# k features of the later batches in 64-row by 32-column tiles of the TensorE array, one matmul for all token tiles, products kept by head pair

## The chip, the cores and the metric

One core of a Trainium2 chip runs the whole program. The metric is device time in microseconds (us), the median of several executions. A profile is taken of one of these executions; its span is about 1.8 us shorter than the time of that execution.

Engine names in the profile: PE is the TensorE matmul, PEld its weight load, DVE is VectorE, ACT is ScalarE, POOL is GpSimd, SP issues most of the DMA. "L256" is line 256 of that kernel's file; the same statement has other line numbers in other versions.

Names in the traces: "pg" and "po" are the results of the matmuls with w_in and w_out, "g" is the square between them, "kvp" collects v^T kp and the sums of kp, "ks" is VectorE's sum of kp over the first eight token tiles, "qT" is q transposed. A "wave" is a group of matmul records that start within a few ns of each other.

## The reference, cut to what matters

```python
batch, n_heads, seq, head_dim = 4, 4, 1088, 32          # r = 8
def phi(x):
    a = einsum('rd,bhsd->bhsr', S1, x)                  # 8 features a
    b = einsum('rd,bhsd->bhsr', S2, x)                  # 8 features b
    return einsum('bhsi,bhsj->bhsij', a, b).reshape(..., 64)
q_p, k_p = phi(q), phi(k)
kv = einsum('bhsf,bhsd->bhfd', k_p, v);  z = k_p.sum(2)
attn = einsum('bhsf,bhfd->bhsd', q_p, kv) / (einsum('bhsf,bhf->bhs', q_p, z)[..., None] + 1e-6)
x = attn as (4352, 128);  h = relu(x @ w_in);  out = (h * h) @ w_out    # w_in 128x2048
```

The feed-forward part (FFN) is by far the larger. Attention for batches 1 to 3 is worked in between its matmuls. This is about one small piece: the features a and b of k ("kf"), their transposes ("fs") and their products ("kp").

## The kernel before: the parts that matter

k lies in `kq`, transposed in blocks of 32: the partitions are the four heads times 32 dimensions, the columns are tokens, `32 * NT = 288` for each of four token groups `p0`. `sk` holds S1 and S2 as block-diagonal weights: head h has rows 32h to 32h+31 and 8 columns of each half.

```python
KG = [[(0, 2), (2, 2), (4, 2), (6, 3)]] + [[(0, 4), (4, 5)]] * (B - 1)   # token tiles per group

def a_kf(b, g, pool, tag):                # batch > 0
    t0, n = KG[b][g]
    kf = pool.tile([128, 512], F32, tag=tag, name="kf")      # one PSUM bank for each token group
    for i in range(2):                    # features a, then features b
        for p0 in range(4):               # four column tiles of the array
            nc.tensor.matmul(
                kf[32 * p0 : 32 * p0 + 32, 32 * n * i : 32 * n * i + 32 * n],
                sk[:, 32 * i : 32 * i + 32],                              # 128 rows x 32 columns
                kq[:, 32 * (NT * p0 + t0) : 32 * (NT * p0 + t0 + n)],
            )
# a_fs: DVE transpose kf -> fs;  a_kp: DVE product kp = a x b, one tile per token group
# [... cut ...]
def a_kf2(b):
    a_kf(b, 0, psa, "feat")               # two banks
    a_kf(b, 1, psa, "tr")

def a_kv(b, t):                           # kvp += v^T kp, token tile t; the last tile has 64 rows
    n, v0, dv = (128, 512 * (t // 4) + 32 * (t % 4), 128) if t < 8 else (64, 1024, 32)
    for h in range(H):
        nc.tensor.matmul(st[b, "kvp"][32 * h : 32 * h + 32, 0:64], vn[b][0:n, ...], kp[0:n, ...], ...)

def loads(n):                             # DMA for batch n, during batch n - 1
    load_qk(kn[n], k, n, 0, S)
    for part in range(3):
        load_v(vn[n], n, part)
    load_qk(qn[n], q, n, 0, S)
```

A small list planner puts every attention task into a numbered FFN step, from estimated durations.

## Time and profile before

| | before |
|---|---|
| time, median of 3 | 202.68 us (202.6 to 203.17) |
| span of the profile | 200.7 us |
| PE busy | 193.1 us (96%) |
| one kf block (from the end of the w_out stream before it to the first FFN matmul after it) | 1.21 us, three times |

From the page of the kernel before: the span, the busy times (engine, us, share, instructions), and the chain of work that ended last, by engine and by line.

```profile
span 200.7 us, 3928 instructions
...
PE 193.1 (96%) x1329; PEld 125.1 (62%) x1329; DVE 143.7 (72%) x375; ACT 144.7 (72%) x326; POOL 50.4 (25%) x225
...
PE 84%; DMA 6%; DVE 3%; ACT 2%; SPq 1%; issue 1%; ACTq 0%
PE po L512 54%; PE pg L489 14%; PE nd L388 7%; DMA w_in_100<-in_moe_w_in_dram 4%; PE qc L362 3%; DMA vn<-in_v_dram 2%; PE kvp L299 2%; PE pt L529 2%; PE kf L256 2%; ACT gt L498 1%; SPq L104 1%; DVE qa L372 1%; PE kvp L310 1%; ACT w_in L684 1%; DVE qp L377 0%
```

PE is the limit. What shares of the chain do not show is whether a microsecond saved on a line is saved at the end. For that one looks for PE gaps after the line: after 20 us there are almost none but those around changes of tile shape. In windows around the three blocks (us, length, then the busy time of PE, PEld, DVE, ACT and POOL with their instructions, the granted clock and the DMA) PE is busy throughout:

```profile
30.00:46.00 16.00, 16.00 (x169) 9.44 (x168) 13.47 (x27) 13.29 (x30) 3.11 (x18) 1.00 0.11 19
...
72.00:88.00 16.00, 16.00 (x169) 9.33 (x168) 14.16 (x30) 12.54 (x28) 0.00 (x0) 1.00 0.25 57
118.00:134.00 16.00, 16.00 (x170) 9.43 (x169) 14.61 (x31) 12.60 (x28) 0.00 (x0) 1.00 0.15 27
```

The chain in order of time (start, us, what) has the three kf blocks:

```profile
33.51 1.12 PE kf L256 x32
...
75.70 1.12 PE kf L256 x32
...
121.29 1.12 PE kf L256 x32
```

The timeline of PE around the first of them (start us, us, what; a merged group starts at its first record):

```profile
32.70 0.81 PE L512 MATMUL po<-g_576,w_o 128*128 128x384 f32 x2
33.44 1.19 PE L256 MATMUL kf<-kq,sk 128*32 128x128 f32 x32
34.56 0.34 PE L489 MATMUL pg<-xT,w_in 128*128 128x384 f16 x1
```

"128*32" is the tile of the array. Each fp32 matmul is two records, so 16 matmuls are 32 records. The groups of instructions that the change touches (count | busy us, mean ns of one | idle before):

```profile
L256 PE MATMUL kf<-kq,sk 128*32 128x160 f32 x48 | 2.2, 299 | 0.0
...
L256 PE MATMUL kf<-kq,sk 128*32 128x128 f32 x48 | 1.9, 279 | 0.0
```

```profile
L282 DVE TENSOR_TENSOR kp<-fs 128x1280 f32<-128x1280 f32 x3 | 4.4, 1483 | 0.0
...
L282 DVE TENSOR_TENSOR kp<-fs 128x1024 f32<-128x1024 f32 x3 | 3.6, 1194 | 0.0
...
L275 DVE STREAM_TRANSPOSE fs<-kf 128x320 f32<-128x320 f32 x3 | 1.5, 499 | 0.0
L275 DVE STREAM_TRANSPOSE fs<-kf 128x256 f32<-128x256 f32 x3 | 1.3, 428 | 0.0
```

The 299 and 279 ns of a kf record are no cost per matmul: four of them run at once and the next four follow 109 or 136 ns later. Costs of packed matmuls are read from the starts of single records.

### The profile page before, as it was taken

The numbers are of one execution on the slowest core, as the hardware profiler recorded it, in microseconds if no ns is written. First come the engines' busy times: TensorE is split into PE (matmuls) and PEld (weight loads), VectorE is DVE, ScalarE is ACT, GpSimd is POOL, SyncE is SP. The second block draws the span as 40 slices with busy tenths as digits, with TensorE's granted clock in tenths as the row PEclk, the third lists the DMA queues.
The fourth block names the chain that finished last, engine by engine and source line by source line (L and its number), as shares of the span: only waits on it lengthen the run. The fifth ranks groups of instructions, "written<-read, shape, count | busy, mean of one in ns | idle before, by whom it ended". The sixth has DMA issues, their size and how long they took to land.

```text
span 200.7 us, 3928 instructions
## 1 busy us (share of the span) xinstructions
PE 193.1 (96%) x1329; PEld 125.1 (62%) x1329; DVE 143.7 (72%) x375; ACT 144.7 (72%) x326; POOL 50.4 (25%) x225
## 2 busy tenths in 40 slices
PE   7998999999999999999999999999999999999990
PEld 2873765567667655667676655667676655556990
DVE  3966966896497669984767788984667767667750
ACT  3428988977696877796978777786888766756730
POOL 3815056000426800001654400000653500000000
PEclk9999999999999999999999999999999999999997
DMA  6699410110120571020112660020122010110201
GB/s 187 184 271 284 141 49 20 20 23 0 23 39 20 164 204 20 2 44 0 36 32 45 207 150 0 3 39 0 23 43 39 2 33 0 22 21 0 39 0 33
DMA packets 31357, 12.34 MB, mean 61 GB/s; under 512 B 23338, under 2 KB 29930, under 8 KB 31338
## 3 DMA queue, kind: packets, MB, share of 16 engines
q1 hardware_dynamic: 30886, 12.00, 24.1%
q8 instruction: 10, 0.16, 0.3%
q10 hardware_dynamic: 452, 0.10, 0.3%
q14 instruction: 9, 0.07, 0.1%
HBM read 8.78 MB, written 2.23 MB: 55 GB/s over the span
## 4 chain that ended last, share of the span: by engine, by line
PE 84%; DMA 6%; DVE 3%; ACT 2%; SPq 1%; issue 1%; ACTq 0%
PE po L512 54%; PE pg L489 14%; PE nd L388 7%; DMA w_in_100<-in_moe_w_in_dram 4%; PE qc L362 3%; DMA vn<-in_v_dram 2%; PE kvp L299 2%; PE pt L529 2%; PE kf L256 2%; ACT gt L498 1%; SPq L104 1%; DVE qa L372 1%; PE kvp L310 1%; ACT w_in L684 1%; DVE qp L377 0%
## 5 line engine op out<-in xcount | busy, mean ns | idle before, releaser
L498 ACT ACTIVATE gt<-pg 128x384 f32<-128x384 f32 (+2 forms) x193 | 88.7, 463 | 34.8 <-PE pg L489 34.0
L544 POOL COPY br<-beta 32x3 f32<-32x3 f32 x192 | 43.5, 227 | 104.4 <-DVE beta L452 97.1
L489 PE MATMUL pg<-xT,w_in 128*128 128x384 f16 (+2 forms) x193 | 61.1, 316 | 0.5 <-ACT gt L498 0.2
L489 PEld LDWEIGHTS <-w_in 128*128 128x128 f16 x193 | 18.9, 98 | 19.1 <-issue 1.4
L372 DVE STREAM_SHUFFLE qa<-qc 128x384 f32<-128x384 f32 x22 | 12.0, 589 | 0.0
L388 PEld LDWEIGHTS nd<-kvz_120,qp 128*128 128x128 f32 x72 | 10.0, 190 | 3.1 <-DVE qp L377 0.3
L388 PEld LDWEIGHTS nd<-kvz_119,qp 128*128 128x128 f32 x72 | 9.9, 190 | 2.5
L377 DVE TENSOR_TENSOR qp<-qa,qb 128x384 f32<-128x384 f32 x22 | 11.2, 544 | 0.0
L552 DVE STREAM_TRANSPOSE oT<-po 128x384 f32<-128x384 f32 (+1 forms) x11 | 6.2, 564 | 6.4 <-PE po L512 6.3
L282 DVE TENSOR_TENSOR kp<-fs 128x512 f32<-128x512 f32 (+3 forms) x10 | 10.7, 1104 | 0.1
L388 PE MATMUL nd<-kvz_120,qp 128*128 128x132 f32 x72 | 10.3, 277 | 0.1
L388 PE MATMUL nd<-kvz_119,qp 128*128 128x132 f32 x72 | 10.0, 277 | 0.0
L404 DVE TENSOR_SCALAR den<-nd 128x12 f32<-128x12 f32 x12 | 2.0, 169 | 10.8 <-PE nd L388 10.7
L362 PE MATMUL qc<-qT,sq 128*128 128x384 f32 x22 | 8.8, 489 | 0.0
L445 DVE TENSOR_TENSOR xs<-nd,sc 128x384 f16<-128x384 f32 (+2 forms) x13 | 6.7, 522 | 0.4
L367 DVE STREAM_SHUFFLE qb<-qc 128x384 f32<-128x384 f32 x11 | 6.5, 588 | 0.0
L299 PE MATMUL kvp<-kp,vn 128*32 128x64 f32 (+1 forms) x288 | 6.3, 222 | 0.0
L299 PEld LDWEIGHTS kvp<-kp,vn 128*32 128x32 f32 (+1 forms) x288 | 4.9, 109 | 2.2 <-DVE ks L322 0.5
L240 DVE STREAM_TRANSPOSE qT<-qn 128x1088 f32<-128x1088 f32 (+2 forms) x5 | 5.3, 1057 | 1.3 <-DMA qn<-in_q_dram 1.3
L409 DVE TENSOR_REDUCE mx<-nd 128x12 f32<-128x384 f32 x12 | 5.9, 495 | 0.0
L362 PEld LDWEIGHTS qc<-qT,sq 128*128 128x128 f32 x22 | 4.1, 190 | 2.8
L558 DVE TENSOR_TENSOR ob<-oT,br 128x384 f32<-128x384 f32 (+1 forms) x11 | 5.8, 530 | 0.0
(702 smaller groups left out, 404.0 us busy)
## 6 DMA issues: line engine op xcount, KB each, us to landing
vn<-in_v_dram SPq DMA_DIRECT2D x32, 64.0 KB, 3.4
kn<-in_k_dram SPq DMA_DIRECT2D x3, 544.0 KB, 7.9
qn<-in_q_dram SPq DMA_DIRECT2D x3, 544.0 KB, 3.6
out_dram<-ob SPq DMA_DIRECT2D x32, 48.0 KB, 1.8
w_in_100<-in_moe_w_in_dram SPq DMA_DIRECT2D x2, 512.0 KB
w_o<-in_moe_w_out_dram SPq DMA_DIRECT2D x2, 512.0 KB, 10.7
out_dram<-ob SPq DMA_DIRECT2D x12, 40.0 KB, 2.6
qn<-in_q_dram SPq DMA_DIRECT2D x1, 352.0 KB
```

The source lines that it names most:

```text
L282: nc.vector.tensor_tensor(out=_ap(kp, 0, 128, 0, [[64, 4 * n], [8, 8], [1, 8]]), in0=_ap(fs, 0, 128, 0, [[8, 4 * n], [1, 8], [0, 8]]), in1 ...
L299: nc.tensor.matmul(st[b, "kvp"][32 * h : 32 * h + 32, 0:64], _ap(vn[b], 0, n, v0 + dv * h, [[1, 32]]), kp[0:n, c0 + 64 * h : c0 + 64 * h + ...
L362: nc.tensor.matmul(qc[:, 0:384], sq[:, :], qT[:, 384 * ch : 384 * ch + 384])
L367: nc.vector.stream_shuffle(in_=st[b, "qc", ch][:, 0:384], out=qb[:, :], mask=mask_b)
L372: nc.vector.stream_shuffle(in_=st[b, "qc", ch][:, 0:384], out=qa[:, :], mask=mask_a[e])
L377: nc.vector.tensor_tensor(out=qp[:, :], in0=st[b, "qa", ch, e][:, :], in1=st[b, "qb", ch][:, :], op=mult)
L388: nc.tensor.matmul(nd[:, 132 * o : 132 * o + 132], st[b, "qp", ch, e][:, 128 * o : 128 * o + 128], st[b, "kvz"][:, 132 * e : 132 * e + 132 ...
L445: nc.vector.tensor_tensor(out=_ap(st[b, "xs", ch], 0, 128, 128 * o, [[32, 4 * n], [1, 32]]), in0=_ap(st[b, "nd", ch], 0, 128, 132 * o, [[3 ...
L489: nc.tensor.matmul(pg[:, c0:c1], w_in[:, 128 * c : 128 * c + 128], st[b, "xT"][:, 384 * ch + c0 : 384 * ch + c1],)
L498: nc.scalar.activation(gt[:, c0:c1], pg[:, c0:c1], Relu)
L512: nc.tensor.matmul(st["po", b, ch][:, c0:c1], w_o[:, 128 * c : 128 * c + 128], g2s[i][1][:, c0:c1], start=first, stop=(c == NFF - 1), skip ...
L544: nc.gpsimd.tensor_copy(_ap(st[b, "br"], 32 * dm, 32, 12 * ch + p0, [[4, 3]]), st[b, "beta"][32 * p0 : 32 * p0 + 32, 3 * ch : 3 * ch + 3],)
```

## The change

Each kf matmul of a later batch contracts over 128 rows although a head needs only 32 of them; the rest of the weights are zeros. The change cuts the array into two row halves as well: heads 0 and 1 in rows 0 to 63, heads 2 and 3 in rows 64 to 127. A half gives 2 heads x 16 = 32 feature columns, one column tile. The banks now belong to head pairs instead of token groups; all nine token tiles go into one matmul of 288 columns, and kp is laid out by head pair. S1 and S2 are interleaved column by column in `sk`, so that a pair's columns are contiguous.

```diff
-    KG = [[(0, 2), (2, 2), (4, 2), (6, 3)]] + [[(0, 4), (4, 5)]] * (B - 1)
+    KG = [[(0, 2), (2, 2), (4, 2), (6, 3)]]
@@ weights
-            _ap(sk, 32 * h, 32, 8 * h, [[32, 2], [1, 8]]),
+            _ap(sk, 32 * h, 32, 16 * h, [[1, 2], [2, 8]]),
@@ a_kf, batch > 0
-            for i in range(2):
-                for p0 in range(4):
-                    nc.tensor.matmul(
-                        kf[32 * p0 : 32 * p0 + 32, 32 * n * i : 32 * n * i + 32 * n],
-                        sk[:, 32 * i : 32 * i + 32],
-                        kq[:, 32 * (NT * p0 + t0) : 32 * (NT * p0 + t0 + n)],
-                    )
+            for p0 in range(4):
+                nc.tensor.matmul(
+                    kf[32 * p0 : 32 * p0 + 32, 0 : 32 * NT],
+                    sk[64 * g : 64 * g + 64, 32 * g : 32 * g + 32],
+                    kq[64 * g : 64 * g + 64, 32 * NT * p0 : 32 * NT * (p0 + 1)],
+                )
@@ products, batch > 0: one tile kp2, by head pair, a and b read at a step of two
+        nc.vector.tensor_tensor(
+            out=_ap(st[b, "kp2"], 0, 128, 128 * NT * g, [[64, 2 * NT], [8, 8], [1, 8]]),
+            in0=_ap(fs, 0, 128, 0, [[16, 2 * NT], [2, 8], [0, 8]]),
+            in1=_ap(fs, 0, 128, 1, [[16, 2 * NT], [0, 8], [2, 8]]),
+            op=mult,
+        )
@@ planner estimates
-        P.add(("kf", n), "PE", 1.2, need, a_kf2, n)
+        P.add(("kf", n), "PE", 0.6, need, a_kf2, n)
[... cut: planner estimates of fs and kp, addresses of kp in kvp and in the ks sums, batch 0's copies at a step of two ...]
```

More of the change, by code (lines that the diff above doesn't have):

```diff
@@ L242, in a_kf @@
     def a_kf(b, g, pool, tag):
-        t0, n = KG[b][g]
+        t0, n = KG[b][g] if b == 0 else (0, NT)
         kf = pool.tile([128, 512], F32, tag=tag, name="kf")
@@ L252, in a_kf @@
         else:
-            for i in range(2):
-                for p0 in range(4):
-                    nc.tensor.matmul(
-                        kf[32 * p0 : 32 * p0 + 32, 32 * n * i : 32 * n * i + 32 * n],
-                        sk[:, 32 * i : 32 * i + 32],
-                        kq[:, 32 * (NT * p0 + t0) : 32 * (NT * p0 + t0 + n)],
-                    )
+            for p0 in range(4):
[4 more added lines that the diff above has]
+                )
         st[b, "kf", g] = kf
     def a_fs(b, g):
-        n = KG[b][g][1]
+        n = KG[b][g][1] if b == 0 else NT
         kf = st[b, "kf", g]
@@ L271, in a_fs, with a_kp2 @@
                     fs[:, 32 * n * i : 32 * n * i + 32 * n],
-                    _ap(kf, 0, 128, 32 * i, [[64, n], [1, 32]]),
+                    _ap(kf, 0, 128, i, [[64, n], [2, 32]]),
                 )
         else:
-            nc.vector.transpose(fs[:, 0 : 64 * n], kf[:, 0 : 64 * n])
+            nc.vector.transpose(fs[:, 0 : 32 * n], kf[:, 0 : 32 * n])
         st[b, "fs", g] = fs
+    def a_kp2(b, g):
+        fs = st[b, "fs", g]
+        if g == 0:
+            st[b, "kp2"] = wpool.tile([128, 2 * 128 * NT], F32, tag="kp2", name="kp2")
+        nc.vector.tensor_tensor(
[4 more added lines that the diff above has]
+        )
     def a_kp(b, g):
@@ L288, in a_kp @@
         for i in range(n):
-            st[b, "kp", t0 + i] = kp, 256 * i
+            st[b, "kp", t0 + i] = kp, [256 * i + 64 * h for h in range(H)]
     def a_kv(b, t):
@@ L295, in a_kv @@
             st[b, "kvp"] = psa.tile([128, 512], F32, tag="acc", bufs=2, name="kvp")
-        kp, c0 = st[b, "kp", t]
+        kp, at = st[b, "kp", t] if b == 0 else (st[b, "kp2"], kp2_at(t))
         n, v0, dv = (128, 512 * (t // 4) + 32 * (t % 4), 128) if t < 8 else (64, 1024, 32)
@@ L301, in a_kv @@
                 _ap(vn[b], 0, n, v0 + dv * h, [[1, 32]]),
-                kp[0:n, c0 + 64 * h : c0 + 64 * h + 64],
+                kp[0:n, at[h] : at[h] + 64],
                 start=(t == 0),
@@ L306, in a_kv, with kp2_at, a_z @@
             )
-    def a_z(b, kp, c0, last):
+    def kp2_at(t, w=128 * NT):
+        return [w * (h // 2) + 128 * t + 64 * (h % 2) for h in range(H)]
+    def a_z(b, kp, at, last):
         for h in range(H):
@@ L312, in a_z @@
                 ones[:, :],
-                kp[:, c0 + 64 * h : c0 + 64 * h + 64],
+                kp[:, at[h] : at[h] + 64],
                 start=False,
@@ L322, in a_ks1 @@
         nc.vector.tensor_tensor(
-            out=ks[:, :], in0=st[b, "kp", 0][0][:, 0:1024], in1=st[b, "kp", 4][0][:, 0:1024],
+            out=_ap(ks, 0, 128, 0, [[512, 2], [1, 512]]),
+            in0=_ap(st[b, "kp2"], 0, 128, 0, [[128 * NT, 2], [1, 512]]),
+            in1=_ap(st[b, "kp2"], 0, 128, 512, [[128 * NT, 2], [1, 512]]),
             op=add,
@@ L328, in a_ks2 @@
         ks = st[b, "ks"]
-        for w in (512, 256):
-            nc.vector.tensor_tensor(
-                out=ks[:, 0:w], in0=ks[:, 0:w], in1=ks[:, w : 2 * w], op=add
-            )
+        for w in (256, 128):
+            lo, hi = (_ap(ks, 0, 128, o, [[512, 2], [1, w]]) for o in (0, w))
+            nc.vector.tensor_tensor(out=lo, in0=lo, in1=hi, op=add)
     def a_kf2(b):
@@ L340, in a_kv9 @@
             a_kv(b, t)
-        a_z(b, *st[b, "kp", 8], False)
-        a_z(b, st[b, "ks"], 0, True)
+        a_z(b, st[b, "kp2"], kp2_at(8), False)
+        a_z(b, st[b, "ks"], kp2_at(0, 512), True)
     def a_kvz(b):
@@ L762 @@
         need = [("kT", n, part) for part in range(3)] + [("qa", n - 1, 2, 1)]
-        P.add(("kf", n), "PE", 1.2, need, a_kf2, n)
+        P.add(("kf", n), "PE", 0.6, need, a_kf2, n)
         for g in range(2):
-            P.add(("fs", n, g), "DVE", 0.4, [("kf", n)], a_fs, n, g)
-            P.add(("kp", n, g), "DVE", 1.15 + 0.3 * g, [("fs", n, g)], a_kp, n, g)
+            P.add(("fs", n, g), "DVE", 0.45, [("kf", n)], a_fs, n, g)
+            P.add(("kp", n, g), "DVE", 1.36, [("fs", n, g)], a_kp2, n, g)
         P.add(("qT", n), "DVE", 1.25, [], a_qT, n, 0, S, first=P.at["kT", n, 2] + 1)
```

## The prediction

> **What bounds the kernel now.** TensorE. The page gives PE busy 193.1 of 200.7 us at full granted clock; 84% of the chain of waits is PE, the k-feature matmuls (kf) 1.7%. VectorE and ScalarE are 72% busy. In windows around the kf blocks (30 to 46, 72 to 88, 118 to 134 us) PE is busy all 16.00 us.
>
> **What one kf block costs.** By single instructions of the trace, batch 1: the last w_out matmul before it starts at 33.02 us and streams about 0.32 us (its spacing to a successor), the first kf matmul starts at 33.44, the first FFN matmul after at 34.56. So the block takes 1.21 us of PE: 0.095 at entry, 32 passes in eight waves of four column tiles (109 ns between waves of 128 columns, 136 ns between waves of 160, together 0.98 us, plus small offsets), 0.10 at exit. The other two blocks look the same. Gaps of 0.09 to 0.10 us also stand around the 64-row matmuls in kvp: a change of tile shape. The Trainium skill, "TensorEngine Tiling (Array Packing)", Key Properties, says that a change of mode drains the array; the trace agrees.
>
> **What changes.** 16 fp32 matmuls (32 passes) per later batch become 8 (16 passes) of 288 columns. If all eight tiles run at once, as the same section says of independent tiles, there are two waves. A wave costs 109/128 = 0.85 ns a column, so 0.245 us. Block: 0.095 + 2 x 0.245 + about 0.07 (eight starts 7 ns apart, the first wave's lag) + 0.10 = 0.75 us (estimate). Saving: 1.21 - 0.75 = 0.46 us per batch, 1.4 us in three. The number of mode changes stays.
>
> Vector work moves without shrinking: transposes 428 + 499 ns become two of about 463; products 1194 + 1483 two of about 1339 (interpolated); the ks additions keep their sizes. By the list planner's arithmetic every task keeps its step and the same 113 squares stay on ScalarE. Batch 0 only gets its columns interleaved: strided small copies, a few ns.
>
> **How much is on the critical path.** All: after 20 us PE has almost no gap but mode changes and 0.67 us at 58.8 to 61.0, where VectorE's qp chain makes it wait; that chain starts from PE's results and shifts with them. The nearest Vector deadlines after kf are the ks sums for kvp: 0.5 us to spare in batch 1, where Vector itself waits for PE after kf and so shifts too, 1.4 us in batch 2, 2.1 us in batch 3. These outlast 0.46 us.
>
> **Prediction.** 202.68 - 1.4 = 201.3 us, range 200.7 to 202.3. Faster by over 2%: 0.01; within: 0.98; slower: 0.01.
>
> **What would show it.** kf: 48 matmul records instead of 96, in two waves of eight, within about 0.6 us; kf share of the chain near 0.9%; FFN steps still 0.81 us apart; kp and fs totals unchanged; span near 199.3.
>
> **What would make it wrong.** If the row halves do not overlap (four waves of 0.245 us), the block stays at 1.2 us and nothing is gained; if only the second pass of g0 overlaps the first of g1, three waves, the gain is about 0.7 us. The skill's "TensorE: Matmul & The Clock Gate", Part 3, calls matmuls strictly in order; today's waves of four, with two passes per tile adjacent in the program, suggest more freedom. A product reading fs at stride two could be slower on VectorE and eat the slack in batch 1.

## The result, and the profile after

| | before | after |
|---|---|---|
| time, median of the 6 runs each of the comparison | 203.19 us (202.6 to 203.45) | 201.13 us (201.05 to 201.87) |
| ratio | | 0.9915, 95% interval 0.9897 to 0.9932 |
| span of the profile | 200.7 us | 199.3 us |
| one kf block | 1.21 us | 0.74 us |

A ratio here compares one kernel with the kernel before in the same rounds; it is not quite the ratio of the quoted medians. The gain of 0.7 to 1.0% is clear of noise. Its size is less sure: the control below measured 0.45 to 0.76% for the same kernel, and the profiles show 1.41 of 200.7 us, 0.7%.

The same parts of the page after:

```profile
span 199.3 us, 3832 instructions
...
PE 192.0 (96%) x1281; PEld 123.2 (62%) x1281; DVE 143.5 (72%) x375; ACT 144.8 (73%) x326; POOL 50.6 (25%) x225
```

The chain of waits after, in order of time:

```profile
33.52 0.65 PE kf L255 x16
...
75.24 0.65 PE kf L255 x16
...
120.37 0.65 PE kf L255 x16
```

Here the gain can be watched as it accumulates. The first block starts at the same time (33.51, now 33.52). From the first to the second it was 42.19 us and is 41.72; from the second to the third 45.59, now 45.13. From the third to the end of the span (200.68 and 199.28 in the trace) 79.39, now 78.91. That is 0.47, 0.46 and 0.48 us, 1.41 in all, and nothing is given back between the blocks.

The timeline of PE after:

```profile
32.71 0.81 PE L526 MATMUL po<-g,w_o 128*128 128x384 f32 x2
33.45 0.72 PE L255 MATMUL kf<-kq,sk 64*32 64x288 f32 x16
34.10 0.34 PE L503 MATMUL pg<-xT,w_in 128*128 128x384 f16 x1
```

The groups after:

```profile
L255 PE MATMUL kf<-kq,sk 64*32 64x288 f32 x48 | 2.1, 415 | 0.0
```

```profile
L281 DVE TENSOR_TENSOR kp<-fs 128x1152 f32<-128x1152 f32 x6 | 7.9, 1341 | 0.1
...
L274 DVE STREAM_TRANSPOSE fs<-kf 128x288 f32<-128x288 f32 x6 | 2.6, 458 | 0.0
```

By means and counts, VectorE's products took 3 x (1483 + 1194) ns = 8.03 us and take 6 x 1341 ns = 8.05; the transposes took 2.78 and take 2.75. (The busy figures 7.9 and 2.6 are lower because instructions that overlap are counted once.) No cost of reading fs at a step of two can be seen, and VectorE's work is as large as before.

The starts of the single kf records of batch 1, in us from the start of the block ("x4": four records 7 ns apart):

| kernel | waves | block |
|---|---|---|
| before | 0.093, 0.227, 0.337, 0.445, 0.554, 0.691, 0.826, 0.962 (x4 each) | 1.213 |
| after | 0.094, 0.361 (x8 each) | 0.743 |

### The profile page after: what moved, and what is told of

The parts are those of the page before. It is cut to its first block, busy times and chain, and to the rows that moved or that the text cites. A ratio compares the mean times of both kernels' runs of the same rounds, so it can differ in the third digit from the quotient of the medians.

```text
span 199.3 us, 3832 instructions
## 1 busy us (share of the span) xinstructions
PE 192.0 (96%) x1281; PEld 123.2 (62%) x1281; DVE 143.5 (72%) x375; ACT 144.8 (73%) x326; POOL 50.6 (25%) x225
## 4 chain that ended last, share of the span: by engine, by line
PE 91%; DVE 4%; ACT 1%; issue 1%; ACTq 0%
PE po L526 54%; PE pg L503 15%; PE nd L402 8%; PE qc L376 3%; PE kvp L309 3%; PE warm L634 2%; PE pt L543 2%; PE rep L651 1%; PE kvp L323 1%; ACT gt L512 1%; PE kf L247 1%; PE kf L255 1%; DVE xs L459 1%; DVE qa L386 1%; DVE qp L391 0%
## 5 line engine op out<-in xcount | busy, mean ns | idle before, releaser
L526 PE MATMUL po<-g,w_o 128*128 128x384 f32 (+3 forms) x386 | 143.9, 458 | 0.0
L526 PEld LDWEIGHTS po<-g,w_o 128*128 128x128 f32 x386 | 66.1, 190 | 32.9 <-issue 21.7
L514 ACT ACTIVATE g<-gt 128x384 f32<-128x384 f32 (+1 forms) x111 | 56.5, 509 | 3.5
L516 DVE TENSOR_TENSOR g<-gt 128x384 f32<-128x384 f32 (+2 forms) x82 | 42.6, 525 | 22.4 <-ACT gt L512 21.6
L402 PEld LDWEIGHTS nd<-kvz,qp 128*128 128x128 f32 x144 | 19.9, 190 | 5.6 <-DVE qp L391 0.3
L402 PE MATMUL nd<-kvz,qp 128*128 128x132 f32 x144 | 20.3, 277 | 0.1
L281 DVE TENSOR_TENSOR kp<-fs 128x1152 f32<-128x1152 f32 x6 | 7.9, 1341 | 0.1
L634 PE MATMUL warm<-zero 128*128 128x512 f16 x13 | 5.0, 550 | 1.2 <-DVE zero L143 1.2
```

The lines of the kernel that those rows point to most:

```text
L402: nc.tensor.matmul(nd[:, 132 * o : 132 * o + 132], st[b, "qp", ch, e][:, 128 * o : 128 * o + 128], st[b, "kvz"][:, 132 * e : 132 * e + 132 ...
L514: nc.scalar.activation(g2[:, c0:c1], gt[:, c0:c1], Square)
L516: nc.vector.tensor_tensor(out=g2[:, c0:c1], in0=gt[:, c0:c1], in1=gt[:, c0:c1], op=mult)
L526: nc.tensor.matmul(st["po", b, ch][:, c0:c1], w_o[:, 128 * c : 128 * c + 128], g2s[i][1][:, c0:c1], start=first, stop=(c == NFF - 1), skip ...
L634: nc.tensor.matmul(t_[:, 0:cols], zero[:, 0:128], zero[:, 0:cols])
```

## The experiments

Theory: the two row halves stream at once, so the array passes 288 columns twice instead of four times, and since PE is the limit this time is saved at the end. Rivals: (A) the gain is half as many, longer matmuls and weight loads; (B) VectorE's re-cut work sets the pace; (C) the gaps around the block are waits for data, not changes of tile shape. A fourth, that the new planner estimates moved tasks, can be put aside: the order of the groups of work on PE, VectorE and ScalarE is the same in the traces before and after, and e1 keeps the new estimates.

The table collects all runs. Whole-kernel times scatter by up to 1 us because the start-up does. So the third column counts from the start of the first kf block to the end of the span in the profile, which leaves the start-up out.

| kernel | median us | first block starts at | from there to the end | ratio to before (95%) |
|---|---|---|---|---|
| before | 203.19 | 33.35 | 167.33 | |
| after | 201.13 | 33.36 | 165.93 | 0.9915 (0.9897 to 0.9932) |
| e1_full_rows | 202.88 | 34.24 | 167.34 | 1.0011 (0.9992 to 1.003) |
| e2_split_tokens | 201.72 | 33.61 | 166.05 | 0.9957 (0.9939 to 0.9974) |
| e3_kf_twice | 202.54 | 33.18 | 167.38 | 1.0004 (0.9986 to 1.0021) |
| e5_v_padded | 200.24 | 33.27 | 165.11 | 0.9884 (0.9868 to 0.99) |
| c_after (control) | 201.39 | 33.39 | 165.93 | 0.9939 (0.9924 to 0.9955) |
| e6_order | 201.76 | 33.37 | 166.35 | 0.9961 (0.9929 to 0.9994) |
| e7_split_halves | 201.27 | 33.42 | 165.93 | 0.9936 (0.9922 to 0.995) |
| e8_q_first | 201.44 | 34.19 | 165.94 | 0.9938 (0.9922 to 0.9953) |
| e9_padded_q_first | 200.54 | 33.81 | 165.13 | 0.989 (0.9874 to 0.9907) |
| e10_before_q_first | 202.56 | 33.25 | 167.36 | 0.9995 (0.9981 to 1.001) |

Runs e1, e2, e3 and e5 shared one chip and one set of runs of the kernel before (median 202.48), c_after, e6 and e7 another (202.64), e8 to e10 a third (202.85). There are six runs of each kernel, but five of e5 and e10 and four of e9. All gave correct results. The experiments e1 to e3 and e5 to e8 are edits of the changed kernel.

### e1_full_rows: the change without row halves

```diff
-                    sk[64 * g : 64 * g + 64, 32 * g : 32 * g + 32],
-                    kq[64 * g : 64 * g + 64, 32 * NT * p0 : 32 * NT * (p0 + 1)],
+                    sk[:, 32 * g : 32 * g + 32],
+                    kq[:, 32 * NT * p0 : 32 * NT * (p0 + 1)],
```

The weights of the other head pair in these 32 columns are zeros, so the result is the same.

> The changed kernel, but each k-feature matmul reads all 128 rows (the weights of the other head pair are zeros), so 8 matmuls of 288 columns in 128 by 32 tiles: same number of instructions as the change, no row halves. Theory (the gain is the two row halves streaming at once): four waves of four tiles, 4 x 0.245 = 0.98 us, block 1.2 us, kernel as before, ratio to before 0.998 to 1.002. Rival (the gain is half as many, longer matmuls and weight loads): block near 0.75 us, ratio near 0.992.

The timeline of PE around the block:

```profile
33.60 0.81 PE L526 MATMUL po<-g,w_o 128*128 128x384 f32 x2
34.34 1.18 PE L255 MATMUL kf<-kq,sk 128*32 128x288 f32 x16
35.45 0.34 PE L503 MATMUL pg<-xT,w_in 128*128 128x384 f16 x1
```

Four waves of four at 0.095, 0.361, 0.604 and 0.847 us, block 1.205 us; 167.34 us from the first block to the end, as before. The same 16 records as the change, the same VectorE work, and the whole gain is gone. Rivals A and B fall. The later waves are 0.243 us apart, 0.84 ns a column, as they are for row halves in e3: a row half streams no faster, there are just two at a time.

### e2_split_tokens: row halves, but the tokens cut again

```diff
-            for p0 in range(4):
-                nc.tensor.matmul(...)                  # 288 columns
+            for c0, c1 in ((0, 128), (128, 32 * NT)):
+                for p0 in range(4):
+                    nc.tensor.matmul(kf[32 * p0 : 32 * p0 + 32, c0:c1], sk[64 * g : ...],
+                        kq[64 * g : 64 * g + 64, 32 * NT * p0 + c0 : 32 * NT * p0 + c1])
```

> The changed kernel, but each 288-column matmul is cut into 128 and 160 columns, as the kernel before cut its tokens: 64-row tiles kept, 16 matmuls per batch again. Theory (row halves): four waves of eight tiles, 2 x 109 + 2 x 136 = 490 ns, block 0.75 to 0.80 us, ratio to before 0.992 to 0.993, as the change itself. Rival (all token tiles in one matmul is what pays): block back at 1.1 to 1.2 us, ratio near 1.0.

Block 0.775 us, so 0.44 of the 0.47 us of the change is kept with twice the matmuls. The ratio missed what was expected (0.9957, its interval begins at 0.9939); the control of the change itself later gave 0.9939, so part of the miss may be that the 0.9915 behind the expectation was low. From the first block to the end it is 166.05 us, 0.12 more than the change, of which three times 0.032 us is the block. In this profile the start-up took 0.26 us longer than in that of the change; why the median of its runs came out higher than this is not settled.

The waves are odd here: 0.095, 0.148, 0.227, 0.281, 0.337, 0.389, 0.473, 0.526, four records each. The second half started 53 ns after the first and stayed behind. e7 asks why.

### e3_kf_twice: the same matmuls issued twice

```diff
+        for _ in range(2):
             for g in range(2):
                 for p0 in range(4):
                     nc.tensor.matmul(...)              # as in the change
```

> The changed kernel with the eight k-feature matmuls of a batch issued twice into the same place. Theory (TensorE is the limit, each microsecond there is a microsecond of the kernel): two more waves in the same tile shape, no more drains, +0.49 us per batch, +1.5 us in all, ratio to before 0.998 to 1.001. Rival (VectorE sets the pace around these blocks and part of the gain came from its re-cut work): the doubled matmuls hide in waits, ratio below 0.996.

The timeline of PE around the block:

```profile
32.53 0.81 PE L534 MATMUL po<-g,w_o 128*128 128x384 f32 x2
33.27 1.20 PE L353 MATMUL kf<-kq,sk 64*32 64x288 f32 x32
34.41 0.34 PE L511 MATMUL pg<-xT,w_in 128*128 128x384 f16 x1
```

The block grows from 0.743 to 1.227 us, and the time from the first block to the end from 165.93 to 167.38, which is +1.45 us for three times 0.484 = 1.45 us. PE time in this block is kernel time, one to one, in this direction too. The whole kernel is back at the time of before (1.0004).

### e5_v_padded: no change of tile shape inside kvp

```diff
         n, v0, dv = (128, 512 * (t // 4) + 32 * (t % 4), 128) if t < 8 else (64, 1024, 32)
+        n = 128 if b > 0 else n
@@ loads
         alloc_loads(n)
+        nc.gpsimd.memset(_ap(vn[n], 64, 64, 1024, [[1, 128]]), 0.0)
```

The unused rows of kp are zeros already (k is padded with zeros), those of v get zeros, so the sum is the same.

> The changed kernel, but the last token tile of kvp in batches 1 to 3 uses 128 rows, with zeros in the empty rows of v, instead of 64 rows: no change of tile shape inside the kvp block. Theory (the 0.09 us gaps are changes of tile shape): both gaps around that tile vanish and the first waves after them lose their lag, about 0.25 us per batch, 0.7 us in all, ratio to before 0.987 to 0.989, against 0.9915 for the change. Rival (the gaps are waits for the load of the last v tile or for the ks sum): the gaps stay, ratio near 0.9915.

The timeline of PE in batch 1's kvp block, in the changed kernel:

```profile
41.31 1.35 PE L309 MATMUL kvp<-kp,vn 128*32 128x64 f32 x72
42.58 0.32 PE L323 MATMUL kvp<-kp,ones 128*32 128x64 f32 x8
42.72 0.29 PE L323 MATMUL kvp<-ks,ones 128*32 128x64 f32 x8
42.95 0.34 PE L503 MATMUL pg<-xT,w_in 128*128 128x384 f16 x1
```

and in this one:

```profile
41.22 1.21 PE L310 MATMUL kvp<-kp,vn 128*32 128x64 f32 x72
42.25 0.29 PE L324 MATMUL kvp<-kp,ones 128*32 128x64 f32 x8
42.36 0.29 PE L324 MATMUL kvp<-ks,ones 128*32 128x64 f32 x8
42.59 0.34 PE L504 MATMUL pg<-xT,w_in 128*128 128x384 f16 x1
```

From the first kvp record to the next FFN matmul it was 1.64 us and is 1.37. In single records, waves follow each other every 0.056 us, but across a change of tile shape every 0.168, and the wave after that in 0.080. Without the two changes all are 0.056. So one change costs about 0.135 us when it stands in a stream of short waves, and rival C falls for this place: the wait of the weight loads for ks is 0.5 us in both profiles, and the gaps are gone. For the kf block no run takes the shape change away; but its entry gap is 0.093 to 0.095 us in all 36 kf blocks of the twelve profiles, which speaks against a wait for data there. Three batches give 0.82 us from the first block to the end (165.93 to 165.11). This kernel beats the one before and the change, at 0.9884.

### c_after, e6_order, e7_split_halves: does the order of issue matter?

The control is the changed kernel again.

> The changed kernel itself once more, as a control beside the next two on one chip: ratio to before 0.990 to 0.994, and from the start of the first k-feature block to the end of the span 165.9 us, as in its first profile, whatever the start-up takes (33.2 to 34.2 us in the profiles so far).

It gave 165.93 us from the first block to the end, as in its first profile, and the ratio 0.9939, within what was expected.

e6 alternates the halves:

```diff
-        a_kf(b, 0, psa, "feat")
-        a_kf(b, 1, psa, "tr")
+        for p0 in range(4):
+            for g in range(2):
+                nc.tensor.matmul(kf[g][32 * p0 : 32 * p0 + 32, 0 : 32 * NT], sk[64 * g : ...], kq[64 * g : ...])
```

> The changed kernel with the two row halves alternating in the order of issue (column tile outside, row half inside). Theory (every tile has its own stream and the engine starts whatever tile is free): still two waves of eight, block 0.74 us, 165.9 us from the first block to the end. Rival (the engine starts matmuls strictly in order of issue, and the change profits from issuing one half after the other): more waves, block above 0.8 us.

Two waves of eight at 0.095 and 0.361 us, block 0.742 us: the order of issue is indifferent here. The trace of the changed kernel says more. In the program as built, the two records of each matmul follow each other, and the first half's eight records stand before the second half's. The semaphore increments that end the first and the second half stand on the fourth and the eighth record of the second wave, none in the first wave. So the first wave holds the first record of every tile, and those of the second half started before the second records of the first half, which were issued earlier.

e7 cuts the tokens as e2 does, but issues both halves' first pieces before the second pieces:

```diff
-            # e2: for g: for (c0, c1): for p0
+            # e7: for (c0, c1): for g: for p0
```

> The split of e2_split_tokens (128 and 160 columns), but both row halves' first pieces issued before the second pieces. In e2 the halves started 53 ns apart, in alternating waves of four, and the block took 0.775 us. If that lag came from the order of issue (the second half's first matmul stands behind the first half's second piece), it goes: waves of eight, block 0.74 to 0.75 us. If it comes from the shorter matmuls, the lag and 0.775 us stay. Whole kernel within 0.2 us of the control either way.

Waves of eight again, at 0.096, 0.229, 0.337 and 0.474 us, block 0.748 us. The 53 ns lag in e2 came from the order of issue: there the second half's first record is the 17th of the block in the program, in e7 and in the change it is the ninth. So a later record can start past busy tiles, but from farther back it came 53 ns late; what sets that is not shown. The cut itself costs 5 ns, so "all token tiles in one matmul" was not what paid.

e6 also showed something that nobody had asked. Its total from the first block to the end is 0.42 us above the control, although the blocks are equal. All of it is lost at 78 us. The timelines there, VectorE of e6:

```profile
76.16 1.31 DVE L240 STREAM_TRANSPOSE qT<-qn 128x1088 f32<-128x1088 f32 x1 [2.32 <-DMA qn<-in_q_dram]
77.39 0.52 DVE L523 TENSOR_TENSOR g<-gt 128x384 f32<-128x384 f32 x1
```

PE of e6:

```profile
77.97 0.91 PE L533 MATMUL po<-g,w_o 128*128 128x384 f32 x2 [0.18 <-DVE g L523]
```

VectorE and PE of the control:

```profile
75.42 1.31 DVE L240 STREAM_TRANSPOSE qT<-qn 128x1088 f32<-128x1088 f32 x1 [1.56 <-DMA qn<-in_q_dram]
76.66 0.52 DVE L516 TENSOR_TENSOR g<-gt 128x384 f32<-128x384 f32 x1
```

```profile
77.64 0.81 PE L526 MATMUL po<-g,w_o 128*128 128x384 f32 x2
```

The bracket gives the idle time before and what ended it. The load of q for batch 2 landed about 0.7 us later in e6; on VectorE an FFN square stands right behind the transpose of q in both kernels, so it was late as well, and PE ran into it. In the kernel before, the same square was done at 77.32 and needed at 78.54, a margin of 1.2 us. In the changed kernel it is done at 76.96 and needed at 77.61: PE's need comes 0.93 us earlier (two saved blocks), the square only 0.36, and 0.65 us of margin are left, 0.48 in the control.

### e8, e9, e10: q loaded ahead of v

```diff
         load_qk(kn[n], k, n, 0, S)
+        load_qk(qn[n], q, n, 0, S)
         for part in range(3):
             load_v(vn[n], n, part)
-        load_qk(qn[n], q, n, 0, S)
```

e8 is this edit on the changed kernel, e9 on e5_v_padded, e10 on the kernel before.

> The changed kernel with the q load of a later batch issued before the v loads instead of after them. In e6_order VectorE stood 2.3 us waiting for q of batch 2, and TensorE lost 0.43 us behind it; in the other profiles the same wait was 1.3 to 1.7 us and cost nothing. Theory (the change brought TensorE's next need closer to that landing, and the slow runs are late landings): the wait for q goes or falls under 0.5 us, from the first k-feature block to the end stays 165.9 us, the runs scatter less (none above 202), median 201.0 to 201.4, ratio to before 0.991 to 0.995. Rival (the scatter is the start-up alone): scatter as in the control, 201.1 to 202.2.

> The version of e5_v_padded with the q load before the v loads: best version so far. From the first k-feature block to the end 165.1 us as in e5, 200.2 us, ratio to before 0.987 to 0.990; the v tile must land early enough, if it does not the kvp block shows a gap and the time rises.

> The kernel before with the q load before the v loads. There the same wait of 1.3 us for q stood 1.2 us ahead of TensorE's need, so taking it away should give nothing: ratio to before 0.998 to 1.002, from the first block to the end 167.3 us. If it gains more than 0.3 us, the late q load was already limiting before the change.

In e8 the wait for q is gone from the list of waits, and the time from the first block is 165.94 us, as expected. But the scatter is not smaller (201.13 to 202.01, control 201.12 to 202.19) and the median is 201.44, just outside what was expected. That points to the rival, start-up: in the profiled run of e8 (201.93 us) the first block starts at 34.19 us, 0.8 us late, and the rest is as long as in the control. e9 is as good as e5 within noise and no better; its median of 200.54 missed the expected 200.2, while ratio and trace were as expected. e10 gains nothing (0.9995), so before the change the late q was not limiting. The edit removes a risk that one profile showed; no gain from it is shown.

What differs in the start-up can be seen from its chain of waits. The changed kernel in its first profile:

```profile
1.22 4.19 PE warm L634 x10
5.41 2.09 PE kf L247 x18
```

and e1_full_rows, whose start-up code is identical:

```profile
1.22 4.45 PE warm L634 x10
5.66 2.73 PE kf L247 x18
```

The same 18 matmuls took 2.09 and 2.73 us. In the changed kernel they follow each other every 0.112 us, in e1 every 0.213 us until about 7.1 us. The 512-column warm-up matmuls show the same step: in the kernel before's profile they start every 0.43 us until about 4 us and every 0.22 us after, in e1 none of the ten is fast. The Trainium skill, "TensorE: Matmul & The Clock Gate", Part 1, gives 426.7 ns cold and 215.7 ns warm for this size; these numbers agree. It says that the change comes around 4 us into sustained matmuls and varies by 0.5 us from run to run; here the traces' clock records put it 2.7 (before) to 5.9 us (e1) after the first warm-up matmul, a wider spread. The three profiles with the latest change (e1 at 7.15 us of the span, e8 at 7.02, e9 at 6.18, the other nine at 3.96 to 5.08) are the three whose first block starts latest (34.24, 34.19, 33.81). Chance, not the edit, makes up to 1 us of difference between two profiles here.

### Not run

A version that keeps the banks by token group, so that both row halves write one bank, was built. The check ahead of the chip refused it: two row tiles of one mode write the same bank and partitions without an order. So what that costs on the chip is open. The Trainium skill, "TensorEngine Tiling (Array Packing)", Restrictions and Gotchas, says: different row tiles cannot use one bank at once. No run here shows it. It is the reason why kp had to move to head pairs.

## Why the prediction was right

- **The limit is PE and the block is on the chain.** Right: 0.47, 0.46 and 0.48 us saved at the three blocks, and e3 shows the same in the other direction.
- **Block of 0.75 us, two waves of eight.** Measured 0.743 us, 0.094 us to the first wave, 0.267 to the second, then 0.382 to the next FFN matmul. The estimate of 0.85 ns a column came from the trace of before and held for 64 rows. The statement of the Trainium skill, "TensorEngine Tiling (Array Packing)", Key Properties, that different tiles can work in parallel held: streaming went from eight waves in 0.98 us to two in 0.49 us (2 x 0.243).
- **Vector work does not shrink.** Products 1341 ns against 1339 interpolated, transposes 458 against 463.
- **Time 201.3 us.** Measured 201.13, and 201.39 in the control. In the profile 199.3 us against the predicted 199.3. The hit to 0.2 us is partly luck: the prediction starts from 202.68, a median of three runs, and in the comparison the kernel before had 203.19, so that the medians differ by 2.06 us and those of the control by 1.25. The 1.4 us that were predicted are what the trace shows where the start-up is left out (167.33 to 165.93).
- **What was missing.** "The nearest Vector deadlines after kf are the ks sums" was not all: the prediction looked at Vector deadlines and forgot a DMA: the load of q, for which VectorE waits before the next square. The margin of the square behind q's transpose fell from 1.2 to 0.65 us (0.48 in the control), and in one profile of a like kernel 0.42 us were lost there. It did not move the median beyond the range.
- **The doubt about strict order** was settled: the places of the semaphore increments show that a later-issued tile starts before an earlier-issued record of a busy tile, and e6 that the order of issue made no difference here.

## What to carry to other kernels

If a small-contraction matmul block lies on a saturated TensorE, count waves: columns per tile times passes, plus about 0.1 us at each change of tile shape, and not the durations of single records. Here cutting the rows in two halved the waves, with the two halves in different PSUM banks, so the layout after the matmul had to follow. The number of matmuls was nearly free (5 ns), their order not quite (32 ns in e2). Before crediting a gain under 1% to a kernel, cut the start-up off: from the first block to the end, like kernels agree to 0.03 us here (e6 apart) where whole times scatter by 1 us.

## What the Trainium skill lacked or had wrong

- "TensorEngine Tiling (Array Packing)", Key Properties: says that a change of mode drains the array, with no price. Here 0.09 to 0.10 us of gap for each, and 0.27 us for two of them within short waves, with the slower first waves after them (e5).
- "TensorE: Matmul & The Clock Gate", Part 3, What overlaps and what doesn't: says that matmuls start and end strictly in order. Here records of eight tiles start in waves whatever the order of issue (0.742 us alternating, 0.743 us half by half), the second half's first records ahead of the first half's second ones. The order is not without effect: 53 ns of lag in e2, none in e7.
- The same page, Part 3, lists measured packings, none of 2 row by 4 column tiles and none that is said to be fp32. Here, against 4 column tiles alone, streaming went from 0.98 to 0.49 us and the block from 1.213 to 0.743 us. "FP8 and Floating Point Precision", TensorE Precision Notes, gives four passes for true fp32; two records of 0.84 ns a column each agree with that at the 2.4 GHz of the other page (estimate: 4 / 2.4 = 1.67 ns).
- No page describes how the granted clock in our profile views can miss the cold start: it reads 1.00 for 0 to 4 us of e1, while the warm-up matmuls are 0.43 us apart; the first clock record of that trace stands at 7.15 us.
